# A nested seven-product scheme for one of the seven gate and up products, with the weights' scaling on VectorE

## The chip, the cores and the metric

The kernel runs on one core of one Trainium2 chip. The metric is the time of one execution on the device in microseconds (us). The kernel before has a median of 1574.11 us in three runs (1573.99 to 1574.41).

The engines are named as in the profile: PE is TensorE (matmuls; PEld its weight loads), DVE is VectorE, ACT is ScalarE, POOL is GpSimd, SP is SyncE, which issues the DMAs.

## The reference

For 2048 rows of 576 columns two branches are computed and mixed by a gate per row. A is attention with 32 heads of 18 columns in four chunks of 512 rows, with a memory carried from chunk to chunk; B is a feed-forward layer with a hidden width of 4608.

```python
def _B_ref(x, w_gate, w_up, w_down):
    return (_gelu(x @ w_gate) * (x @ w_up)) @ w_down

x = A_x
g = _sigmoid((x * gate_w).sum(-1, keepdims=True))
a = _A_ref(x, A_wq, A_wk, A_wv, A_wo, A_beta)
b = _B_ref(x, B_w_gate, B_w_up, B_w_down)
return g * a + (1 - g) * b
```

The change is in B's gate and up products, `x @ w_gate` and `x @ w_up`, and in what the two branches share.

## The kernel before

Every f32 operand is held as two 16-bit words, high and low, and a product is three matmuls (high by high, high by low, low by high) that add up in PSUM. ACT writes the high words (a copy to f16), POOL or DVE the low words (the value less its high word).

**Steps and blocks.** The hidden width is 36 tiles of 128, called f; the 2048 rows are four chunks of 512. A step `step(v)`, v = 0 to 71, does one f tile (f = v // 2) for one pair of chunks (p = v % 2): gate and up for two chunks. Four steps make a block (fb = v // 4, i4 = v % 4), with two f tiles. A step also holds a pair of attention heads (`scores`, `powers`, `pair_rows`, `turn_rows`, `values`) and a quarter of the down products of the block before (`chains`: `early` and `late`, six matmuls of 288 columns each into one bank, added to `acc` by DVE).

**Seven products.** The four products of a step (gate and up by two chunks), each over 512 inner columns, are formed with seven block products after Strassen's scheme (Winograd's form). Their weights are parts of `pairg`: A11, A22, S1, S2, S3, S4 and A12 by sums made on POOL (`sums_g`), from gate and up weights that were first scaled on POOL (`scale_g`, and `scale_d` for the down weights). The chunk side has its sums too (tile `xt`). Each product is six matmuls of 512 columns (`product`). The 64 columns beyond 512 are done by `rest` and `low_rests`. The S3 product starts each step in bank V (`first_product`), and DVE copies V out as g1 before the other products add to the bank.

**Order.** The instructions stand on each engine in the order in which the program issues them; each engine runs its own list in order and waits by semaphores. So the place of an instruction among the others of its engine is set by the place of its line in `step`. The helpers `weights_first`, `weights_high` (ACT), `weights_low` (POOL) and `weights_load` (SP) prepare the weights of the next tiles in fixed steps of a block: i4=1 and i4=3 have `sums_g`, i4=0 and 2 `scale_g`, i4=2 and 3 `scale_d`, `high_d`, `low_d`.

**Attention beside it.** `scores` puts four matmuls into PSUM; its pieces (`put`) let DVE add the mask, take the maximum and write the f32 probabilities' tile `pf`; `powers` is ACT's exp in place; `pair_rows` writes high and low words into the tile `ph`; `turn_rows` lets SP turn both by two DMA transposes into `pt`, which `values` multiplies. At a step's start, ACT runs the exps that the step before issued last.

**Other names.** `hh` are the high and low words of the hidden values (tiles of one pool for each parity of f), `gl` f32 hidden values in three homes, `raw` and `rawd` the f32 weights as loaded, `paird` the down weights' words, `acc` the f32 result, `ob` and `oh` the attention's result and its words (`result_high`, `result_low`), `squares` sums of squares that give the next weights' scales.

Of the kernel before, what the change touches and what calls it, by code (L numbers as in the profile page):

```python
# [18 lines left out]
P = 128  # L19
D = 576  # L20
F = 4608
H = 32
# [13 lines left out]
GB = 17  # L36
# [7 lines left out]
def kernel(ctx: ExitStack, tc: tile.TileContext, xs, wqk, wv, wo, wgu, wd, beta, out):  # L44
# [34 lines left out]

    def sum_squares(o, r):  # L80
        junk = wts.tile([P, KT * P], BF16, name="junk", tag="junk", bufs=1)
        dve.tensor_tensor_reduce(junk[:, : r.shape[1]], r, r, 1.0, 1e-30, OP.mult, OP.add, o)

    def act_square(o, r):
        junk = wts.tile([P, KT * P], BF16, name="junk", tag="junk", bufs=1)
        act.activation(junk[:, : r.shape[1]], r, AF.Square, accum_out=o)
# [208 lines left out]
    A11, A12, U4, A22, G4, S3, S1, UG, S2, S4 = 0, 2, 4, 5, 7, 8, 10, 12, 13, 15  # L295
    KW = KT * P

    def scale_g(f):
        if f >= NF:
            return  # L300
        for i in (1, 0):
            r = raw_g[f][:, i * KW : (i + 1) * KW]
            pool.tensor_scalar(r, r, scl[f // 2][0][:, 0:1], None, OP.mult)  # L303

    def parts_g(f, b):

        if f >= NF:
            return ()
        if b:
            return ((0, KW, S3), (KW, KW + 4 * P, S2))  # L310
        return ((KW, 2 * KW, A11), (2 * P, KW, A22))
# [6 lines left out]
    def sums_g(f):  # L318
# [6 lines left out]
        pool.tensor_tensor(g0, u0, g0, OP.subtract)  # L325
# [13 lines left out]

    def scale_d(f):  # L340
        r = raw_d[f]
        pool.tensor_scalar(r, r, scl[f // 2 + 1][0][:, 1:2], None, OP.mult)
# [44 lines left out]
    def form_sums(p, i, half, by=dve):  # L387
# [4 lines left out]
        if t is not None:  # L392
            hi, lo = (flat(t[:, 4 * k + j : 4 * k + j + 2]) for j in (0, 2))
        if half <= 0:
            by.tensor_tensor(r[o], r[a], r[b], OP.subtract)
        if half == 0 or half == 2:
            act.activation(hi, r[o], AF.Copy, scale=sc)
        if half == 1:
            dve.scalar_tensor_tensor(lo, r[o], sc, hi, OP.mult, OP.subtract)
# [19 lines left out]
    gh = cst.tile([P, 2, H], F32, name="gh")  # L419
# [14 lines left out]

    first, stay = ExitStack(), ctx.enter_context(ExitStack())
    with tc.tile_pool(name="prj", bufs=2, side="right", reuse_waits="tile") as pp:
        al = pp.tile([P, 4, 3], F32, name="al", bufs=1)
        nal = pp.tile([P, 4, 2], F32, name="nal", bufs=1)
        unq = pp.tile([P, 1], F32, name="unq", bufs=1)
# [4 lines left out]
        xt = [mp.tile([P, 12, L], F16, name="xt0", bufs=1)]  # L444
# [225 lines left out]
        with tc.manual_schedule(engines=ORDERED):  # L670
# [60 lines left out]
            for i in range(2):  # L731
                fold_squares(0, i)
# [68 lines left out]
            def beside_products(s, j):  # L801
# [4 lines left out]
                if s == 0:  # L806
                    if j == 0:
# [3 lines left out]
                        make_qk(3, pair_low)  # L811
                    if j == 1:
# [4 lines left out]
                        outscale(0, 2)  # L817
                        make_qk(4)
# [21 lines left out]
                if s == 2:  # L840
# [5 lines left out]
                    if j == 3:  # L846
                        load_sums(1)
                    if j == 8:
                        for f in range(3):
                            load_g(f)  # L850
                if s == 3:
# [3 lines left out]
                    if j == 1:  # L855
                        high_g(0, 1)
                        low_g(0, 1)
# [3 lines left out]
                    if j == 4:  # L861
                        load_g(3)
                    if j == 6:
# [8 lines left out]
                    if j == 8:  # L872
                        high_g(1, 1)
# [9 lines left out]
            for s in range(4):  # L883
# [26 lines left out]
                for j in range(9):  # L910
# [14 lines left out]
                    if s == 3 and j == 1:  # L925
# [3 lines left out]
                        xt.append(mp2.tile([P, 12, L], F16, name="xt1", bufs=1))  # L929
                        home.update(r=mp2)  # L930
                    beside_products(s, j)
# [25 lines left out]
    with tc.tile_pool(name="keep", bufs=2, side="right", reuse_waits="tile") as kp, ExitStack() as tail:  # L957
# [66 lines left out]
        def powers(a):  # L1024
# [5 lines left out]
            for qi in (3, 0, 2, 1):  # L1030
# [3 lines left out]
        def pair_rows(a, i):  # L1034

            p = prob[a]
            if i == 0:
                pairs16[a] = ap_.tile([P, 2, 10 * P], F16, name="ph", bufs=2)
# [3 lines left out]
            act.activation(h[:, 0, cols], p[:, cols], AF.Copy)  # L1042
            pool.tensor_tensor(h[:, 1, cols], p[:, cols], h[:, 0, cols], OP.subtract)  # L1043

        def turn_rows(a):
            prob.pop(a)
            t, h = turned_p[a], pairs16.pop(a)
            for i in range(2):
                sp.dma_start(t[:, 10 * i : 10 * i + 10], h[:, i], transpose=True)
# [34 lines left out]
        def result_high(gg):  # L1084
            ob = obs[gg]
            oh = ohs[gg] = ap_.tile([P, 2, 8, 4 * DH], F16, name="oh", bufs=1)
            act.activation(flat(oh[:, 0]), flat(ob), AF.Copy, scale=wsc[:, 3:4])

        def result_low(gg):
            hf, g = divmod(gg, H // 4)  # L1090
            ob, oh = obs.pop(gg), ohs.pop(gg)
            dve.scalar_tensor_tensor(flat(oh[:, 1]), flat(ob), wsc[:, 3:4], flat(oh[:, 0]), OP.mult, OP.subtract)
            d0 = g * 4 * DH
            for i in range(2):
                for a, b, c in ((d0, min(d0 + 4 * DH, 4 * P), i * 4 * P), (max(d0, 4 * P), d0 + 4 * DH, (4 + i) * P - i * 64)):
                    if a < b:
                        sp.dma_start(oas[hf][:, c + a : c + b].rearrange("(t p) c -> p t c", p=P),
                                     oh[:, i, :, a - d0 : b - d0])
# [19 lines left out]
        def chains(b, js):  # L1118
            for j in js:
                down(b, j // 2, j % 2)  # L1120
                if j % 8 == 7:
                    for ff in (2 * b, 2 * b + 1):
                        hp.pop((ff, j // 8))
                        if j == 31:
# [7 lines left out]
        def hidden_pair(f, c, t):  # L1132
            hh = hp[f, c] = (kp if f % 2 else mp2).tile([P, 2, L], F16, name=f"hh{f % 2}", bufs=6 - 2 * (f % 2))
# [40 lines left out]

# [22 lines left out]
        def act_squares(v):  # L1197

            fb, i4 = divmod(v, 4)
            todo = {0: ((fb + 1, 2 * fb, 2),),  # L1200
                    1: ((fb + 1, 2 * fb + 3, 0), (fb + 1, 2 * fb + 3, 1), (fb + 1, 2 * fb + 1, 2)),
                    2: ((fb + 2, 2 * fb + 4, 0), (fb + 2, 2 * fb + 4, 1))}
            todo = todo.get(i4, ()) if fb else ()
            if v == 4:
# [6 lines left out]
        def first_product(v):  # L1211
            f, p = divmod(v, 2)
            V = bank("V")
            product(V, f, S3, xt[p], 8, 10, True)
            g1 = gl_tile()
            dve.tensor_copy(g1, V)  # L1216
            return V, g1

# [14 lines left out]
        def step(v):  # L1233
# [12 lines left out]
            low = (k - 8) // 4 if k % 4 == 0 and 0 <= (k - 8) // 4 < H // 2 - 1 else None  # L1246
# [381 lines left out]
```

## Time and profile before

| | before |
|---|---|
| median of three runs | 1574.11 us |
| profiled execution, own time | 1574.38 us |
| its span in the trace | 1572.5 us |
| granted clock of PE | 1.00 |
| first step of block 0 | starts at 214.1 us |
| a block in the steady state | 73.15 us |
| its steps | 18.25 us each, the step i4=1 18.40 us |

The span is taken from the first to the last instruction in the trace, 1.9 us less than the execution's own time. A row of the timeline gives start, length, engine, line, operation, tiles and count; the length of a row with a count is from the first start to the last end, and matmuls overlap, so that PE's time is read from start to start. A row of a group gives the count, the busy time, the mean length of one in ns, and the idle time of the engine ahead of them with its releaser. The stretch shown in the prediction, from 750.87 us, is one steady step with i4=3; the steps ahead of it start at 714.22 (i4=1) and 732.62 (i4=2), the next one at 769.11 (i4=0).

### The profile page before, as it was taken

The page shows a single profiled execution, that of the slowest core. Times are in us where ns is not written, and L with a number is a line of the kernel's source. Part 1 is how long each engine was busy: PE and PEld are TensorE (multiplying, and loading weights), DVE is VectorE, ACT ScalarE, POOL GpSimd, SP SyncE. Part 2 cuts the span into 40 slices and gives each one's busy share as a digit, 9 for nine tenths or more (in the row PEclk, how much of TensorE's full clock was granted, in tenths as well). Part 3 has the DMA queues.
Part 4 walks back from the last instruction along what each step waited for, and adds up shares of the span by engine and source line. Part 5 has one row for each costly group of instructions (what it writes and reads, how often), then busy time and mean ns, then how long its engine had stood idle before and what let it go on. Part 6 is the DMA issues. An engine that isn't in the chain of part 4 may idle for free.

```text
span 1572.5 us, 32751 instructions
## 1 busy us (share of the span) xinstructions
PE 1562.6 (99%) x11914; PEld 929.0 (59%) x11914; DVE 1150.2 (73%) x3027; ACT 1172.7 (75%) x1983; POOL 1229.6 (78%) x1180
## 2 busy tenths in 40 slices
PE   9999999999999999999999999999999999999999
PEld 5665754555555555555555555555555555555577
DVE  6778974777777776767777777777777777776565
ACT  7566544988888888888888888888888888886421
POOL 4254765888888879898987888887879797788697
PEclk9999999999999999999999999999999999999999
DMA  6632432678788788978887888888797988884644
GB/s 228 215 123 101 149 120 72 111 129 128 134 135 136 127 151 125 139 127 138 129 131 129 139 133 137 133 134 152 131 136 129 144 129 136 129 127 91 135 108 136
DMA packets 472825, 209.88 MB, mean 133 GB/s; under 512 B 427688, under 2 KB 437416, under 8 KB 472152
## 3 DMA queue, kind: packets, MB, share of 16 engines
q1 hardware_dynamic: 472664, 207.80, 72.6%
q8 instruction: 93, 1.52, 0.4%
q14 instruction: 68, 0.56, 0.1%
HBM read 91.87 MB, written 27.26 MB: 76 GB/s over the span
## 4 chain that ended last, share of the span: by engine, by line
PE 95%; DVE 2%; ACT 1%; issue 1%; POOL 1%; DMA 0%; SPq 0%; ACTq 0%
PE dn L1108 27%; PE U L1148 18%; PE V L1148 12%; PE G L1148 12%; PE pv L1063 4%; PE dn L367 2%; PE U L1155 2%; PE st L360 2%; PE G L1160 1%; PE V L1160 1%; PE st L1016 1%; PE st L1468 1%; PE G L1155 1%; PE V L1155 1%; PE U L360 1%; PE dn L1016 1%
## 5 line engine op out<-in xcount | busy, mean ns | idle before, releaser
L1043 POOL TENSOR_TENSOR ph<-pf,ph 128x512 f16<-128x512 f32 (+1 forms) x256 | 353.6, 1402 | 173.2 <-ACT ph L1042 173.2
L1108 PE MATMUL dn<-paird,hh 128*128 128x288 f16 x3396 | 476.5, 286 | 0.0
L1148 PEld LDWEIGHTS <-pairg 128*128 128x128 f16 x3024 | 285.3, 98 | 305.1 <-issue 19.0
L1108 PEld LDWEIGHTS <-hh 128*128 128x128 f16 x3456 | 331.8, 98 | 153.7 <-issue 18.0
L1116 DVE SCALAR_TENSOR_TENSOR acc<-dn,ev,acc 128x288 f32<-128x288 f32 x534 | 274.4, 515 | 53.9 <-PE dn L1108 43.9
L1032 ACT ACTIVATE pf<-pf,mb,esc 128x512 f32<-128x512 f32 (+3 forms) x512 | 292.9, 642 | 7.0 <-POOL ph L1043 0.4
L1148 PE MATMUL U<-xt,pairg 128*128 128x512 f16 x864 | 210.0, 379 | 0.0
L1148 PE MATMUL G<-x,pairg 128*128 128x512 f16 x864 | 210.0, 379 | 0.0
L1135 POOL TENSOR_TENSOR hh<-gl,hh 128x512 f16<-128x512 f32 x144 | 164.3, 1160 | 19.1 <-ACT hh L1134 19.1
L338 POOL TENSOR_TENSOR pairg<-raw,pairg 128x640 f16<-128x640 f32 (+2 forms) x144 | 175.4, 1239 | 4.1 <-ACT pairg L334 4.1
L334 ACT ACTIVATE pairg<-raw 128x640 f16<-128x640 f32 (+2 forms) x144 | 90.0, 650 | 114.6 <-POOL raw L328 66.6
L1042 ACT ACTIVATE ph<-pf 128x512 f16<-128x512 f32 (+1 forms) x256 | 172.5, 721 | 0.0
L1293 DVE COPY gl<-U 128x512 f32<-128x512 f32 x72 | 49.8, 692 | 167.3 <-POOL hh L1135 150.8
L1019 DVE CUSTOM_DVE_ANT_0 pf<-st,mask 128x512 f32<-128x512 f32 (+1 forms) x256 | 157.2, 614 | 0.0
L303 POOL TENSOR_SCALAR raw<-raw,sc 128x640 f32<-128x640 f32 x72 | 135.7, 1896 | 0.0
L1019 DVE CUSTOM_DVE_ANT_0 pf<-dn,mask 128x256 f32<-128x256 f32 (+1 forms) x192 | 67.2, 375 | 81.7 <-PE dn L1016 81.7
L1138 ACT ACTIVATE gl<-gl,sc 128x512 f32<-128x512 f32 x144 | 96.6, 715 | 37.4 <-DVE gl L1319 19.3
L1148 PE MATMUL V<-xt,pairg 128*128 128x512 f16 x432 | 105.7, 381 | 0.0
L1148 PE MATMUL V<-x,pairg 128*128 128x512 f16 x432 | 104.8, 378 | 0.7 <-DVE gl L1216 0.7
L1148 PE MATMUL U<-x,pairg 128*128 128x512 f16 x432 | 105.0, 379 | 0.0
L1134 ACT ACTIVATE hh<-gl 128x512 f16<-128x512 f32 x144 | 82.6, 616 | 15.8 <-DVE gl L1130 15.7
L1063 PEld LDWEIGHTS <-pt 128*128 128x128 f16 x2560 | 83.4, 96 | 6.3
(316 smaller groups left out, 2642.6 us busy)
## 6 DMA issues: line engine op xcount, KB each, us to landing
raw<-in_wgu_dram SPq DMA_DIRECT2D x36, 640.0 KB
rawd<-in_wd_dram SPq DMA_DIRECT2D x36, 288.0 KB
qt<-qk SPq DMA_DIRECT2D x132, 72.0 KB
kt<-qk SPq DMA_DIRECT2D x132, 72.0 KB
qk<-stage SPq DMA_DIRECT2D x36, 256.0 KB
qt<-qk SPq DMA_DIRECT2D x132, 36.0 KB
kt<-qk SPq DMA_DIRECT2D x132, 36.0 KB
vp<-vstage SPq DMA_DIRECT2D x16, 296.0 KB
```

The lines of the kernel that those rows point to most:

```text
L303: pool.tensor_scalar(r, r, scl[f // 2][0][:, 0:1], None, OP.mult)
L338: pool.tensor_tensor(spot(f, *p, 1), raw_g[f][:, p[0] : p[1]], spot(f, *p, 0), OP.subtract)
L1019: dve.tensor_tensor_reduce(prob[a][:, COL[qi] : COL[qi + 1]], out[qi], mask[:, L - (qi + 1) * P :], 1.0, -3e38, OP.add, OP.max, mx[a][:, q ...
L1032: act.activation(r, r, AF.Exp, bias=b[:, qi : qi + 1], scale=esc[:, 0, c : c + 1])
L1042: act.activation(h[:, 0, cols], p[:, cols], AF.Copy)
L1043: pool.tensor_tensor(h[:, 1, cols], p[:, cols], h[:, 0, cols], OP.subtract)
L1063: pe.matmul(ov, pr[:, 10 * i + COL[qi] // P + kb], v[:, 4 * e + kb, c0 : c0 + VC], start=kb == 0 and i == 0, stop=kb == qi and i == 1)
L1108: pe.matmul(o[:, :NH], hh[:, a, q * P : (q + 1) * P], w[:, b, n * NH : (n + 1) * NH], start=i == 0, stop=i == 5)
L1116: dve.scalar_tensor_tensor(av, o[:, :NH], ev, av, OP.mult, OP.add)
L1135: pool.tensor_tensor(hh[:, 1], t, hh[:, 0], OP.subtract)
L1138: act.activation(t, o, AF.Gelu_apprx_tanh, scale=scl[f // 2][0][:, 2 + c : 3 + c])
L1148: pe.matmul(o, w[:, i, (a + k) * P : (a + k + 1) * P], x[:, b + k], start=start and k == 0 and i == 0 and b == h, stop=k == 1 and i == 1, ...
```

## The change

The S3 product of two f tiles of a block and one chunk pair is now done at once, as a 2 by 2 block product in its own right: seven products of 256 columns (three matmuls each) in place of two times six matmuls of 512 columns. Its weights (seven blocks: W00, W01, W11 and the sums WS1 to WS4, high and low words) lie in a new tile `nest`; the chunk side has seven blocks of 256 columns in `xt`. The pieces `nest(at, 0)` to `nest(at, 4)` stand in the steps i4=3 (for p = 0 of the next block) and i4=0 (for p = 1), the last one at the start of the following step. They gather their result in bank V for the even f and in an f32 tile `hold` for the odd f, whose g0 is then Y plus `hold`. Block 0 has no nest: its S3 product is 15 matmuls of 256 columns.

The parts that the prediction speaks of:

```diff
+    def nest_odd(b):
+        if b < NB:
+            nest_w[b] = nest_tile()
+            r = raw_g[2 * b + 1]
+            pool.tensor_tensor(nest_part(b)[1], r[:, KW : KW + 2 * P], r[:, : 2 * P], OP.subtract)
+
+    def nest_pairs(b, i, what):
+        if b >= NB:
+            return
+        a, r = nest_part(b)
+        src, o = ((a, W00), (r[:, P:], W11), (r, WS3), (a, WS2))[i]
+        n = src.shape[1]
+        hi, lo = (nest_w[b][:, (o + 7 * j) * P : (o + 7 * j) * P + n] for j in range(2))
+        if "h" in what:
+            act.activation(hi, src, AF.Copy)
+        if "l" in what:
+            pool.tensor_tensor(lo, src, hi, OP.subtract)
...
     def scale_d(f):
         r = raw_d[f]
-        pool.tensor_scalar(r, r, scl[f // 2 + 1][0][:, 1:2], None, OP.mult)
+        dve.tensor_scalar(r, r, scl[f // 2 + 1][0][:, 1:2], None, OP.mult)
...
             h = pairs16[a]
-            cols = (slice(6 * P, 10 * P), slice(0, 6 * P))[i]
-            act.activation(h[:, 0, cols], p[:, cols], AF.Copy)
-            pool.tensor_tensor(h[:, 1, cols], p[:, cols], h[:, 0, cols], OP.subtract)
+            cols = (slice(0, 6 * P), slice(6 * P, 10 * P))[i]
+            act.activation(h[:, cols], p[:, cols], AF.Copy)
+            pool.tensor_tensor(p.bitcast(F16)[:, cols], p[:, cols], h[:, cols], OP.subtract)
...
         def weights_first(fb, i4):
             n0 = 2 * fb
-            if i4 == 0 and fb:
-                scale_g(n0 + 1)
-            if i4 == 1 and fb:
+            if i4 == 0:
+                scale_g(n0 + 1, BACK)
+            if i4 == 1:
                 sums_g(n0 + 1)
-            if i4 == 2 and fb:
+            if i4 == 2:
                 scale_g(n0 + 2)
+                scale_g(n0 + 3, FRONT)
                 scale_d(n0)
-            if i4 == 3 and fb:
-                sums_g(n0 + 2)
+            if i4 == 3:
                 scale_d(n0 + 1)
+
+        def weights_nest(fb, i4, late):
+            if i4 == 2 and late:
+                sums_g(2 * fb + 2)
+                nest_odd(fb + 1)
+            if i4 == 3 and not late:
+                for i in range(2):
+                    nest_pairs(fb + 1, i, "hl")
+                nest_sums(fb + 1)
+            if i4 == 3 and late:
+                for i in (2, 3):
+                    nest_pairs(fb + 1, i, "hl")
...
+            if n == 0:
+                nest_product(b, A, WS3, XT3, p, True)
+                dve.tensor_copy(h1, A)
+                nest_product(b, B, W00, X00, p)
+            if n == 1:
+                nest_product(b, A, W11, XT4, p)
+                dve.tensor_copy(h0, A)
+                dve.tensor_copy(A, B)
+            if n == 2:
+                nest_product(b, B, W01, X10, p)
+                nest_product(b, A, WS2, XT2, p)
+                dve.tensor_tensor(h0, A, h0, OP.add)
+            if n == 3:
+                nest_product(b, A, WS1, XT1, p)
+                dve.tensor_tensor(h1, A, h1, OP.add)
+            if n == 4:
+                nest_product(b, A, WS4, X11, p)
...
             if fb:
                 weights_high(fb, i4)
                 weights_low(fb, i4)
+                weights_nest(fb, i4, True)
...
             product(Y, f, S4, x2_, 2, 6)
             rest(Y, f, UG, x2_, (0,) if fb else (0, 1))
+            nest(at, 0)
             some(fb - 1, late[:1])
...
-            some(fb - 1, late[1:])
+            some(fb - 1, late[1:2])
+            nest(at, 1)
+            some(fb - 1, late[2:])
             if low is not None:
                 result_low(low)
             if on(k - 1):
                 values(2 * k - 2)
+            nest(at, 2)
...
             if on(k):
                 puts[2 * k + 1] = scores(2 * k + 1)
+            nest(at, 3)
```

Beside these: `pairg` has 15 parts instead of 17; the result's low words lie in `ob`, and `result_low` moves from i4=0 to i4=3; `hh` tiles come from one list of eight homes; `powers` and `pair_rows` take their parts in another order; the squares of a block's first `rawd` move from i4=0 to i4=1; `fold_squares(0, ...)` stands later in the prologue; the output stage holds fewer tiles ahead.

On POOL, step i4=3 of a steady block, from the sums or the nest's words to the last words of the step. Before (`raw` are weights' sums, `ph` probabilities' words):

```order
L324 TENSOR_TENSOR raw<-raw 128x256
L325 TENSOR_TENSOR raw<-raw 128x256
L326 TENSOR_TENSOR raw<-raw 128x256
L327 TENSOR_TENSOR raw<-raw 128x256
L328 TENSOR_TENSOR raw<-raw 128x128
L342 TENSOR_SCALAR rawd<-rawd,sc 128x576
L1043 TENSOR_TENSOR ph<-pf,ph 128x512
L1043 TENSOR_TENSOR ph<-pf,ph 128x768
L338 TENSOR_TENSOR pairg<-raw,pairg 128x640
L338 TENSOR_TENSOR pairg<-raw,pairg 128x512
L350 TENSOR_TENSOR paird<-rawd,paird 128x576
```

And of the changed kernel, the same step (L377 are the nest's low words, L384 to L387 its sums, L1141 the probabilities' low words):

```order
L377 TENSOR_TENSOR nest<-raw,nest 128x256
L377 TENSOR_TENSOR nest<-nest 128x128
L384 TENSOR_TENSOR nest<-nest 128x128
L385 TENSOR_TENSOR nest<-raw,nest 128x128
L386 TENSOR_TENSOR raw<-nest,raw 128x128
L387 TENSOR_TENSOR raw<-raw 128x128
L1141 TENSOR_TENSOR pf<-pf,ph 128x768
L1141 TENSOR_TENSOR pf<-pf,ph 128x512
L342 TENSOR_TENSOR pairg<-raw,pairg 128x384
L342 TENSOR_TENSOR pairg<-raw,pairg 128x512
L399 TENSOR_TENSOR paird<-rawd,paird 128x576
L377 TENSOR_TENSOR nest<-nest 128x256
```

The scaling has left the list and the weights' sums have moved to the step ahead; four of the nest's sums and two of its low words stand at the place of the sums, and the low words of WS3, the last row, behind all other words of the step.

On DVE, step i4=2 of a steady block, from the copy of X to Y to what follows the last piece of a `put`. Before:

```order
L1257 COPY U<-G 128x512
L1116 SCALAR_TENSOR_TENSOR acc<-dn,ev,acc 128x288
L1019 ISA pf,mx<-st,mask 128x384
L1019 ISA mx 128x1
L1293 COPY gl<-U 128x512
```

And of the changed kernel:

```order
L1426 COPY U<-G 128x512
L1215 SCALAR_TENSOR_TENSOR acc<-dn,ev,acc 128x288
L1117 ISA pf,mx<-st,mask 128x384
L1117 ISA mx 128x1
L304 TENSOR_SCALAR raw<-raw,sc 128x1280
L304 TENSOR_SCALAR raw<-raw,sc 128x2x256
L391 TENSOR_SCALAR rawd<-rawd,sc 128x576
L1475 TENSOR_TENSOR gl<-U,hold_11823 128x512
```

Three scalings stand between the last piece and g0, and g0 is a sum with `hold` instead of a copy.

More of the change, by code (lines that the diff above doesn't have):

```diff
@@ L35 @@
 VC = 2 * DH + 1
-GB = 17
+GB = 15
 MC = DH + 1
@@ L1217, in first_product, with nest_product, nest @@
             return V, g1
+        nested, holds = {}, {}
+        def nest_product(b, o, i, j, p, start=False):
+            w, x = nest_w[b], x_block(p, j)
+            for n, (c, d) in enumerate(((0, 0), (0, 1), (1, 0))):
+                pe.matmul(o, w[:, (7 * c + i) * P : (7 * c + i + 1) * P], x[d], start=start and n == 0, stop=n == 2,
+                          skip_group_check=True)
+        def nest(at, n):
+            if at is None:
+                return
+            b, p = at
+            if n == 0:
+                nested[at] = bank("V")
+                holds[p] = kp.tile([P, L], F32, name=f"hold{p}", bufs=1)
+            B, A = (nested[at][:, i * HX : (i + 1) * HX] for i in range(2))
+            h0, h1 = (holds[p][:, i * HX : (i + 1) * HX] for i in range(2))
+            if n == 0:
+                nest_product(b, A, WS3, XT3, p, True)
[14 more added lines that the diff above has]
+                nest_product(b, A, WS4, X11, p)
         ends, puts = [], {}
@@ L1252, in step @@
             act_squares(v)
-            V, g1 = ahead.pop(v) if v in ahead else first_product(v)
+            at = (fb + 1, 0) if i4 == 3 and fb + 1 < NB else (fb, 1) if i4 == 0 and fb else None
+            if not fb:
+                V, g1 = ahead.pop(v) if v in ahead else first_product(v)
+            elif i4 < 2:
+                if on(k - 2):
+                    values(2 * k - 3)
+                nest((fb, p), 4)
+                V, g1 = nested.pop((fb, p)), gl_tile()
+                dve.tensor_copy(g1, V)
+            else:
+                V, g1 = bank("V"), holds[p]
+                product(V, f, A22, x2_, 0, 4, True)
             X, Y = bank("G"), bank("U")
@@ L1259, in step @@
                 last_sum(1, 1)
+                for i in range(2):
+                    nest_pairs_x(1, i)
             if v == 1:
@@ L1540 @@
             NT = 8
-            for t in range(turned_n, 11):
+            for t in range(turned_n, 9):
                 turned(t)
```

202 lines of the change are left out of this document (144 added, 58 removed).

## The prediction

> **What bounds the kernel now.** I read the shares of the page first, then the chain that ended last, then TensorE's waits.
>
> ```profile
> PE 1562.6 (99%) x11914; PEld 929.0 (59%) x11914; DVE 1150.2 (73%) x3027; ACT 1172.7 (75%) x1983; POOL 1229.6 (78%) x1180
> PE 95%; DVE 2%; ACT 1%; issue 1%; POOL 1%; DMA 0%; SPq 0%; ACTq 0%
> ```
>
> TensorE is busy 99% of the span and carries 95% of the chain. Its waits by releaser add up to a few microseconds, each of them met once; the only one in the feed-forward loop is
>
> ```profile
> PE V L1148 <- DVE gl L1216: 0.7, 1, 0.7
> ```
>
> So before the change a matmul removed is time removed. But the other engines are at 73 to 78%, and POOL's work comes in bursts, so the steady state has to be read step by step. One block of two f tiles is four steps (i4 = 0 to 3). I use the block around 751 us; its step i4=3 runs from 750.87 to 769.11. The window view of that step (span, then busy time and instructions of PE, PEld, DVE, ACT, POOL, then clock) says:
>
> ```profile
> 750.87:769.11 18.24, 18.24 (x149) 10.60 (x147) 13.06 (x37) 14.44 (x24) 16.37 (x16) 1.00 0.71 118
> ```
>
> PE never stops, POOL is busy 16.37 of 18.24 us, and the clock is full. PE's timeline of the step:
>
> ```profile
> 750.87 1.47 PE L1148 MATMUL V<-xt,pairg 128*128 128x512 f16 x6
> 752.17 1.46 PE L1148 MATMUL G<-x,pairg 128*128 128x512 f16 x6
> 757.51 0.90 PE L1108 MATMUL dn<-paird,hh 128*128 128x288 f16 x6
> 758.25 1.46 PE L1148 MATMUL G<-x,pairg 128*128 128x512 f16 x6
> 762.32 0.38 PE L1016 MATMUL st<-kt,qt 54*128 54x512 f16 x2
> 762.69 1.65 PE L1108 MATMUL dn<-paird,hh 128*128 128x288 f16 x12
> 765.47 0.38 PE L1155 MATMUL U<-x,pairg 128*128 128x512 f16 x1
> 765.68 2.40 PE L1108 MATMUL dn<-paird,hh 128*128 128x288 f16 x18
> ```
>
> From start to start, six 512-column matmuls take 1.30 us (216 ns each) and six of 288 columns 0.74 us (123 ns).
>
> **Term 1, matmuls.** For blocks 1 to 17 the S3 product, the first row above, leaves all four steps: 24 x 216 ns = 5.2 us a block. The nested product puts 2 x 21 matmuls of 256 columns there. No row has that width. By columns from 512 it is 108 ns, from 288 it is 109; the ceiling is the 123 ns of 288 columns. I take 109: 4.6 us. Saved: 0.6 us a block (0.0 at the ceiling), 17 x 0.6 = 10 us. Block 0 goes from 6 x 216 to 15 x 109 ns in four steps, +0.34 us each, +1.4 us. Net about -9 us if nothing waits. It also shifts PE within the block: i4=1 and 2 lose 1.30 us each (about 17 us long), while i4=3 and 0 keep their length, the nest's pieces standing late in i4=3.
>
> **Term 2, POOL in step i4=3.** The new weights of the nested product (sums and seven pairs of high and low words) are made in i4=2 and 3, just ahead of their use. POOL executes in order. The third matmul of nest piece 0 needs the low words of WS3, and in the changed order these stand behind POOL's whole list of step i4=3. When is that list done? It starts where it starts today, with the probabilities' low words after ScalarE's exps and high words:
>
> ```profile
> 751.01 2.29 ACT L1032 ACTIVATE pf<-pf,mb,esc 128x512 f32<-128x512 f32 x4
> 753.21 1.35 ACT L1042 ACTIVATE ph<-pf 128x512 f16<-128x512 f32 x2
> 753.90 2.77 POOL L1043 TENSOR_TENSOR ph<-pf,ph 128x512 f16<-128x512 f32 x2 [1.64 <-ACT ph L1042]
> 758.85 0.73 POOL L324 TENSOR_TENSOR raw<-raw 128x256 f32<-128x256 f32 x1
> 759.66 0.72 POOL L325 TENSOR_TENSOR raw<-raw 128x256 f32<-128x256 f32 x1
> 769.27 1.28 POOL L350 TENSOR_TENSOR paird<-rawd,paird 128x576 f16<-128x576 f32 x1
> ```
>
> POOL starts 3.0 us into the step; with the 768 columns first, 3.2. I keep this start: ScalarE's own list for the shorter i4=2 fills it, so exps do not come earlier. The durations, by form:
>
> ```profile
> L1043 POOL TENSOR_TENSOR ph<-pf,ph 128x768 f16<-128x768 f32 x128 | 210.5, 1644 | 0.0
> L1135 POOL TENSOR_TENSOR hh<-gl,hh 128x512 f16<-128x512 f32 x144 | 164.3, 1160 | 19.1 <-ACT hh L1134 19.1
> L338 POOL TENSOR_TENSOR pairg<-raw,pairg 128x512 f16<-128x512 f32 x36 | 41.8, 1160 | 0.0
> L338 POOL TENSOR_TENSOR pairg<-raw,pairg 128x384 f16<-128x384 f32 x36 | 33.4, 928 | 0.0
> L350 POOL TENSOR_TENSOR paird<-rawd,paird 128x576 f16<-128x576 f32 x36 | 46.1, 1281 | 6.3 <-ACT paird L346 6.3
> L324 POOL TENSOR_TENSOR raw<-raw 128x256 f32<-128x256 f32 x36 | 26.2, 727 | 0.2
> L328 POOL TENSOR_TENSOR raw<-raw 128x128 f32<-128x128 f32 x36 | 16.3, 454 | 0.0
> ```
>
> In the order of the new list: probabilities 1.64 + 1.16; hidden low words 2 x 1.16; nest low words of 256 and 128 columns 0.73 + 0.45; nest sums 4 x 0.45, with four gaps of 0.08 (758.85 to 759.66 for 0.73); probabilities 2.80; pairg 0.93 + 1.16; paird 1.28; at last the WS3 low words 0.73. That is 15.3 us, less some 0.2 for neighbours that overlap in the timeline: done about **18.3 us** into the step.
>
> PE wants them early. Today the U product closes at 765.68, 14.8 us into the step; without the S3 product that is 13.5, and the third nest matmul stands 0.2 behind it: **13.7 us**. The difference, **4.6 us**, is a wait in every block, with late chains, values, scores and the block's end queued behind it on PE. Today POOL ends its list as late (769.27 + 1.28, 19.7 us after the step's start) and nobody notices, since those words serve the next block. The time is a constant one, not made good by the step's end: the next exps hang on the gelu of this step, and that on PE. Scaling by VectorE does take 1.7 us out of this list, and the sum has it out. Bounds of this term: 4.0 (ScalarE half a microsecond early) to 6.5 (ScalarE late by a microsecond, and the locks below). Sixteen steps have it (blocks 1 to 16 make the nest of the next): 16 x 4.6 = 74 us.
>
> **Term 3, block 0 to 1.** Step v=3 has no late chains between the nest's pieces; copies and adds of 256 columns, each half of a 512-column VectorE copy, lie bare between matmuls, and WS3 comes late there too.
>
> ```profile
> L1257 DVE COPY U<-G 128x512 f32<-128x512 f32 x72 | 50.0, 695 | 2.6 <-PE G L1148 2.6
> ```
>
> Five of 0.35 to 0.7 us, and 1.5 for the weights: 3 to 5 us, bounds 0 and 8. I take 4.
>
> **Term 4, VectorE's new scales.** No f32 tensor_scalar from SBUF to SBUF of this size is in the trace. By the copy's 695 ns per 512 columns, the 2368 columns of i4=2 are 3.2 us; at half of that, 1.6. They stand ahead of g0's add, which S1 on PE needs, where VectorE is idle today:
>
> ```profile
> 757.81 0.69 DVE L1293 COPY gl<-U 128x512 f32<-128x512 f32 x1 [2.38 <-POOL hh L1135]
> ```
>
> So 1.6 are hidden, 3.2 stick out by 0.8, and PE would wait for some of it. There is a second price, a lock between VectorE and POOL. Beside VectorE's tensor_scalar at 177.96, two POOL rows (640 and 384 columns) that take 1.43 and 0.93 alone took 3.48:
>
> ```profile
> L338 POOL TENSOR_TENSOR pairg<-raw,pairg 128x640 f16<-128x640 f32 x72 | 103.3, 1434 | 4.1 <-ACT pairg L334 4.1
> 177.96 1.41 DVE L228 TENSOR_SCALAR x<-x,xr 128x4608 f16<-128x4608 f16 x1
> 178.02 3.48 POOL L338 TENSOR_TENSOR pairg<-raw,pairg 128x640 f16<-128x640 f32 x2 [2.41 <-ACT pairg L334]
> ```
>
> That is 1.1 us more than alone, while VectorE's instruction ran on for 1.3. In i4=2 a scale may have to let a POOL row of up to 1.64 us go first. Range 0 to 1.4 us a block; I take 0.2, since most of it lies in the idle 2.38 us.
>
> **Term 5, low words in place.** The probabilities' low words now lie in pf itself, so VectorE's next mask-and-max into that buffer waits for the DMA transposes out of it. Their issue in i4=0:
>
> ```profile
> 774.05 5.92 SPq L1049 DMA_TRANSPOSE pt<-ph  x2
> ```
>
> It ends 10.9 us into that step; the scores (762.32, 11.4 us into their step) come 0.8 to 1.3 us earlier than now, and one chain later PE wants the bank that VectorE is to empty. Nothing if they land at once, 1.1 us if they need the 1.4 us more that I allow; 0.2 a block.
>
> The rest costs nothing: squares and exps only change places on ScalarE, which is not waited for; the tail's smaller buffers lie beside PE work; the later folds may give 0.7 us in the prologue.
>
> **The sum**, against the profiled execution's 1574.4 (span 1572.5; the median 1574.1 is 0.3 below): 1574.4 - 9 + 74 + 4 + 17 x 0.4 = **1650 us**.
>
> [...]
>
> **The rivals.**
> - POOL is in time (faster). If POOL's list began 4.6 us earlier, or WS3's place in it were no matter, only the matmuls would count: 1574.4 - 9 = **1565**. For it: POOL loses all its scaling:
>
> ```profile
> L303 POOL TENSOR_SCALAR raw<-raw,sc 128x640 f32<-128x640 f32 x72 | 135.7, 1896 | 0.0
> L342 POOL TENSOR_SCALAR rawd<-rawd,sc 128x576 f32<-128x576 f32 x36 | 62.0, 1722 | 0.0
> ```
>
> These are 198 us, and it gains some 58: 17 nests of 4 x 0.73 + 5 x 0.45 us, less 36 x 0.5 by narrower low words and 17 x 0.73 by a sum left out. The point that decides is 13.7 us into i4=3. Against it: the start of the list is set by exps, not by POOL's load, and fifteen microseconds stand ahead of WS3. Chance 0.15.
> - The wait is there but 1 to 2.5 us, by ScalarE running ahead in i4=2: 1574.4 - 9 + 4 + 16 x 1.75 = **1597**. Chance 0.15.
> - Locks and the transposes bite fully: +0.6 in i4=3, 1.2 more in i4=2 and 0.9 more in i4=0, 16 x 2.7 over the sum, **1693**. For it: the rows at 178 us. Against it: VectorE's idle time. Chance 0.10.
> - The change doesn't do what it says: a 256-column matmul costs 123 ns. Then term 1 is +1 instead of -9: 1660 with the waits, 1575 without them. Chance of the latter 0.03.
>
> **The numbers.** The forecast, waits of 4 to 6 us in i4=3, has 0.57. Its own range is 1635 to 1675. The range that should hold the time 8 times in 10 takes in the partial wait and the locks: 1585 to 1695. A measurement of this kernel can tell about 0.2% from no change. Faster by more 0.15, within 0.03, slower by more 0.82.
>
> **What would show it.** TensorE's waits should have a row for nest behind POOL's low words (L377) of about 4.6 us x 16, and POOL's timeline should have its last-but-one nest row ending 18 us after i4=3's start; steps i4=1 and 2 should be near 17 us. Term 1 is read from the starts of the nest's rows (109 ns). If that wait is under 1 us, term 2 is wrong, and POOL's start or ScalarE's place is where to look. If waits stand behind the scales (L304, L391) or behind transposes, terms 4 or 5 were too small.

## The result and the profile after

| | before | after |
|---|---|---|
| median | 1574.26 us (four runs, 1573.99 to 1574.54) | 1745.96 us (four runs, 1744.47 to 1746.91) |
| span of the profiled execution | 1572.5 us | 1745.2 us |
| granted clock of PE, mean | 1.00 | 0.976 |

The changed kernel is slower: the ratio of the times is 1.109, with a 95% interval of 1.1076 to 1.1104. That is 172 us, where 76 were forecast, and outside the range.

The shares of the engines, on the page of the changed kernel:

```profile
PE 1613.6 (92%) x12256; PEld 977.2 (56%) x12256; DVE 1292.8 (74%) x3256; ACT 1183.1 (68%) x2057; POOL 1120.5 (64%) x1218
```

PE went from 99% to 92%, so it now waits; yet its busy time grew by 51 us with less work to do, which no count of matmuls explains. POOL is less busy than before. The waits of PE, by releaser (total, times, longest):

```profile
PE V L1346 <- POOL nest L377: 68.4, 16, 4.8
PE V L1346 <- DVE hold L1361: 19.9, 34, 0.8
PE U L1249 <- DVE gl L1475: 5.9, 16, 0.4
PE G L1249 <- DVE gl L1230: 5.6, 33, 0.2
PE dn L1207 <- DVE mx L1117: 4.0, 5, 1.1
PE dn L1207 <- DVE acc L1215: 3.0, 15, 0.2
```

The first row is term 2 of the prediction, sixteen times. The second was in no term: the copy of A out of the bank, twice a block. (The profile counts 0.58 us of idleness for each; from start to start it costs 0.75 us.)

Measured from the end of one step's scores to the next, the steady steps last, by their means, 18.24 us (i4=1, before 18.40), 17.74 (i4=2, 18.25), 25.74 (i4=3, 18.24) and 20.70 (i4=0, 18.26): a block went from 73.15 to 82.42 us. By stretches, the way up to the end of the first step with attention grew by 16.0 us (the prologue ahead of the first block product by 7.8 of them), the 63 steps behind it by 148.7, and the way from there to PE's last matmul by 7.7.

One long wait on PE's timeline, and POOL's at the same place:

```profile
1249.73 0.38 PE L1256 MATMUL U<-x,pairg 128*128 128x512 f16 x1
1249.95 0.38 PE L1346 MATMUL V<-xt,nest 128*128 128x256 f16 x2
1254.83 0.28 PE L1346 MATMUL V<-xt,nest 128*128 128x256 f16 x1 [4.50 <-POOL nest L377]
1255.70 0.80 PE L1346 MATMUL V<-xt,nest 128*128 128x256 f16 x3 [0.58 <-DVE hold L1361]
1256.29 0.92 PE L1207 MATMUL dn<-paird,hhd 128*128 128x288 f16 x3
1257.01 0.92 PE L1207 MATMUL dn<-paird,hhr 128*128 128x288 f16 x3
...
1258.82 0.49 PE L1346 MATMUL V<-xt,nest 128*128 128x256 f16 x3
1259.15 0.53 PE L1207 MATMUL dn<-paird,hhd 128*128 128x288 f16 x3
1259.52 0.53 PE L1207 MATMUL dn<-paird,hhr 128*128 128x288 f16 x3
```

```profile
1239.72 2.98 POOL L1141 TENSOR_TENSOR pf<-pf,ph 128x768 f16<-128x768 f32 x2 [0.79 <-ACT ph L1140]
...
1247.64 0.46 POOL L387 TENSOR_TENSOR raw<-raw 128x128 f32<-128x128 f32 x1
1248.06 2.88 POOL L1141 TENSOR_TENSOR pf<-pf,ph 128x768 f16<-128x768 f32 x2
1250.90 2.02 POOL L342 TENSOR_TENSOR pairg<-raw,pairg 128x384 f16<-128x384 f32 x2
1252.88 1.27 POOL L399 TENSOR_TENSOR paird<-rawd,paird 128x576 f16<-128x576 f32 x1
1254.11 0.67 POOL L377 TENSOR_TENSOR nest<-nest 128x256 f16<-128x256 f32 x1
```

The step begins at about 1236.5. POOL's list starts 3.2 us later and its WS3 words are done at 1254.78, 18.3 us later; PE's third nest matmul, due at 1250.17, starts at 1254.83. Both ends are the forecast's, 18.3 and 13.7. What was not forecast follows in the same rows: the fourth matmul stops again, for VectorE's copy, and the down products behind it go from start to start in 0.72 us by threes (240 ns each), before they return to 0.37 (122 ns). In the window view of PE (the window and its length, PE's busy time and matmuls, the granted clock, the share of the DMA engines and GB/s):

```profile
1252.00:1254.00 2.00, 0.00 (x0) 1.00 0.73 164
1254.00:1256.00 2.00, 0.58 (x3) 0.76 0.37 82
1256.00:1258.00 2.00, 2.00 (x11) 0.50 0.77 214
1258.00:1260.00 2.00, 2.00 (x20) 0.89 0.46 179
1260.00:1262.00 2.00, 1.94 (x35) 1.00 0.00 0
```

After 4.5 us without a matmul PE runs on at half its clock for 3.4 us (what the three windows with 0.76, 0.50 and 0.89 lack of the full clock, taken twice). This is one part of how its busy time grew; the experiment that fills the wait, below, puts it at about half of the 51 us.

### The profile page after: what moved, and what is told of

Its sections match the earlier page's. It is cut to its first block, busy times and chain, and to the rows that moved or that the text cites. A ratio compares the mean times of both kernels' runs of the same rounds, so it can differ in the third digit from the quotient of the medians.

```text
span 1745.2 us, 34088 instructions
## 1 busy us (share of the span) xinstructions
PE 1613.6 (92%) x12256; PEld 977.2 (56%) x12256; DVE 1292.8 (74%) x3256; ACT 1183.1 (68%) x2057; POOL 1120.5 (64%) x1218
## 5 line engine op out<-in xcount | busy, mean ns | idle before, releaser
L1141 POOL TENSOR_TENSOR pf<-pf,ph 128x768 f16<-128x768 f32 (+1 forms) x256 | 368.2, 1438 | 418.9 <-ACT ph L1140 408.9
L1207 PE MATMUL dn<-paird,hhr 128*128 128x288 f16 x2124 | 341.8, 295 | 3.8 <-DVE acc L1215 2.0
L1130 ACT ACTIVATE pf<-pf,mb,esc 128x256 f32<-128x256 f32 (+3 forms) x512 | 292.9, 642 | 5.5 <-issue 0.4
L1207 PEld LDWEIGHTS <-hhr 128*128 128x128 f16 x2160 | 214.6, 101 | 103.8 <-issue 13.3
L1207 PE MATMUL dn<-paird,hhd 128*128 128x288 f16 x1272 | 213.1, 294 | 3.4 <-DVE mx L1117 2.4
L1346 PE MATMUL V<-xt,nest 128*128 128x256 f16 x714 | 121.6, 285 | 92.6 <-POOL nest L377 68.4
L1140 ACT ACTIVATE ph<-pf 128x768 f16<-128x768 f32 (+1 forms) x256 | 172.4, 720 | 0.0
L342 POOL TENSOR_TENSOR pairg<-raw,pairg 128x384 f16<-128x384 f32 (+2 forms) x144 | 156.4, 1108 | 12.9 <-ACT pairg L338 12.9
L1207 PEld LDWEIGHTS <-hhd 128*128 128x128 f16 x1296 | 128.6, 100 | 58.3 <-issue 8.3
L1236 POOL TENSOR_TENSOR hhr<-gl,hhr 128x512 f16<-128x512 f32 x67 | 79.9, 1203 | 23.4 <-ACT hhr L1235 23.4
```

What stands on the lines that cost most here:

```text
L342: pool.tensor_tensor(spot(f, *p, 1), raw_g[f][:, p[0] : p[1]], spot(f, *p, 0), OP.subtract)
L1130: act.activation(r, r, AF.Exp, bias=b[:, qi : qi + 1], scale=esc[:, 0, c : c + 1])
L1140: act.activation(h[:, cols], p[:, cols], AF.Copy)
L1141: pool.tensor_tensor(p.bitcast(F16)[:, cols], p[:, cols], h[:, cols], OP.subtract)
L1207: pe.matmul(o[:, :NH], hh[:, a, q * P : (q + 1) * P], w[:, b, n * NH : (n + 1) * NH], start=i == 0, stop=i == 5)
L1236: pool.tensor_tensor(hh[:, 1], t, hh[:, 0], OP.subtract)
```

## The experiments

Each time below is that of a single run. The kernel before, run beside each, took 1573.99 to 1574.93 us; the four runs of the changed kernel differ by up to 2.4 us, so a difference of that size between two of these times shows nothing by itself.

### The place of the WS3 words in POOL's list

First, the nest's last words ahead of the weights' low words:

```diff
                 turn_rows(2 * k - 1)
+            if fb and i4 == 3:
+                weights_nest(fb, i4, True)
...
                 weights_low(fb, i4)
-                weights_nest(fb, i4, True)
+                if i4 != 3:
+                    weights_nest(fb, i4, True)
```

Second, also ahead of the odd head's probabilities, directly behind the nest's sums (ScalarE's high words move to the same places; the last hunk is as above, and a step without an odd head has the words too):

```diff
                 powers(2 * k - 1)
+                if fb and i4 == 3:
+                    weights_nest(fb, i4, True)
                 pair_rows(2 * k - 1, 0)
```

> The low words of WS3 stand behind the probabilities' low words but ahead of the three last weights' rows (0.93 + 1.16 + 1.28 us). If their place in POOL's list makes PE wait, TensorE's wait behind the nest's low words falls from 4.65 to about 1.3 us a block, 16 x 3.4 = 54 us. If TensorE's clock falls to a half because it had been idle over 4 us, that goes too, 1.4 us a block, 22 us more: about 1670. Without a share of the clock 1692. If POOL as a whole is late, the wait only moves: about 1745.

> The low words of WS3 and WS2 stand directly behind the nest's sums, ahead of the odd head's probabilities. By the place in POOL's list the wait behind the nest is gone (16 x 4.65 = 74 us, and 22 of the clock): about 1650. If the odd head's low words, now 2.5 us later in that step, reach their DMA transposes too late, VectorE waits for these at the next step's start and gives back 1 to 2 us a block: 1666 to 1680.

Measured: 1682.99 us and 1657.46 us. The row of waits behind the nest in the first:

```profile
PE V L1346 <- POOL nest L377: 16.4, 14, 1.3
```

The single wait fell by just the three rows of POOL that were passed, to at most 1.3 us; in the second the row is gone, and with it 88 us. The wait on POOL is thus a matter of place, as argued. In the first the time lies between the two figures for the clock: its mean clock is 0.99, not 1.00. In four blocks this wait (1.45 us from start to start) and the copy's 0.75 directly behind it were still followed by the half clock, in most not. In the second, a part came back as a wait of the nest's piece 3 for VectorE's sums:

```profile
PE V L1346 <- DVE hold L1370: 6.2, 12, 0.8
```

### The copy between A and B

```diff
                 nest_product(b, A, WS3, XT3, p, True)
-                dve.tensor_copy(h1, A)
                 nest_product(b, B, W00, X00, p)
+                dve.tensor_copy(h1, A)
```

> Only the order in the nest's first piece is changed: the copy of A out of bank V stands behind B's three matmuls instead of ahead of them. If B's first matmul waits for that copy because both lie in one bank, 34 waits of 0.75 us go: about 1746 - 25 = 1721. If the matmuls are slow there for another reason (VectorE's turn, clock), nothing changes: 1745.

Measured: 1730.05 us; of the 34 waits for the copy one of 0.5 us is left. So B's first matmul waited, by the program's semaphores, for a copy of the other half of its bank; whether the chip itself would need that wait is not shown. The step i4=0 gained 0.79 us, the step i4=3 only 0.17, and 9 us of the forecast are missing: there the half clock lasted longer instead. The trace's record of the clock has it for 6.8 us in 14 of the 16 blocks here, in the changed kernel for 6.8 us in 7 and for 3.4 us in 9 (mean clock 0.969 against 0.976). The two orders together, the second kernel above with this edit:

> The early WS3 words and the copy behind B together. If the two costs are apart from each other (the wait on POOL with its half clock, and the wait on VectorE's copy), they add up: 1657.5 - 33 x 0.75 = 1633. If the copy's place only matters beside the long wait, it stays near 1657.

Measured: 1633.29 us. Once the long wait is gone, the copy's whole price shows: 24.2 us below the second kernel of the first experiment.

### Filling the wait

```diff
+                if b > 1 and p == 0:
+                    for _ in range(40):
+                        pe.matmul(A, nest_w[b][:, WS3 * P : (WS3 + 1) * P], x_block(p, XT3)[0], start=True, stop=False,
+                                  skip_group_check=True)
                 nest_product(b, A, WS3, XT3, p, True)
```

> In the sixteen steps with the long wait TensorE repeats the nest's first matmul 40 times (40 x 0.109 = 4.4 us) while POOL works; each repeat starts the sum anew. If the half clock after the wait comes from TensorE's idleness, it stays at 1.00 and the kernel gets faster by about 16 x 1.4 = 22 us, to about 1724, although it does more. If it is not the idleness, the time stays at 1745 or grows.

Measured: 1728.64 us, 17 us less than the changed kernel with 640 matmuls more. PE's timeline and the clock behind the same place:

```profile
1241.08 4.53 PE L1362 MATMUL V<-xt,nest 128*128 128x256 f16 x40
1245.44 0.81 PE L1346 MATMUL V<-xt,nest 128*128 128x256 f16 x3
1246.84 0.49 PE L1346 MATMUL V<-xt,nest 128*128 128x256 f16 x3 [0.58 <-DVE hold L1365]
1247.16 0.53 PE L1207 MATMUL dn<-paird,hhd 128*128 128x288 f16 x3
```

```profile
1246.00:1248.00 2.00, 1.42 (x11) 1.00 0.71 173
1248.00:1250.00 2.00, 2.00 (x29) 1.00 0.81 236
```

The forty matmuls take 4.36 us from start to start (109 ns each, the value taken in term 1), POOL's words come as late as ever, and the chains behind run at full clock. PE's busy time is 1658.3 us, which less 640 matmuls of 109 ns is 25 us below that of the changed kernel. So the half clock was the price of PE's idleness, and a wait of this length costs more than itself. Its price is 1.5 us a block, 24 us in all, more than the 17 us won: the steady step i4=3 lasts 24.22 us (25.74 without the filling), but for one of 29.43 us, in which PE waits 3.75 us for VectorE's masks. In the sixteen waits of the changed kernel, after 3.3 to 4.8 us of idleness, the slow matmuls (240 ns for 288 columns) begin 1.0 to 1.9 us after PE resumed and end 3.2 to 6.5 us after it. But shorter idleness was enough at times, as the four blocks above show (1.45 and 0.75 us from start to start).

### Parts of the change alone, in the kernel before

The weights' scaling on VectorE (two words changed, `pool` to `dve`, in `scale_g` and `scale_d`); the output stage's sums written over their own inputs; the probabilities' low words in place (with the changed order of the parts); and the first with the third.

```diff
-            pool.tensor_tensor(s1, a21, a22, OP.add)
-            pool.tensor_tensor(s2, s1, a11, OP.subtract)
-            pool.tensor_tensor(s3, a11, a21, OP.subtract)
-            pool.tensor_tensor(s4, a12, s2, OP.subtract)
+            pool.tensor_tensor(a22, a21, a22, OP.add)
+            pool.tensor_tensor(a21, a11, a21, OP.subtract)
+            pool.tensor_tensor(a11, a22, a11, OP.subtract)
+            pool.tensor_tensor(a12, a12, a11, OP.subtract)
...
-            pool.tensor_tensor(h[:, 1, cols], p[:, cols], h[:, 0, cols], OP.subtract)
+            pool.tensor_tensor(p.bitcast(F16)[:, cols], p[:, cols], h[:, cols], OP.subtract)
```

> The kernel before, with only the weights' scaling moved from POOL to VectorE (at the same places, 2 x 640 and 576 columns). If the scales delay g0's copy and the sums behind it, PE waits 0.5 to 0.9 us in i4=2 as in the changed kernel: 1574 + 17 x 0.5 to 0.9 = 1583 to 1589. If VectorE's idle 2.4 us and POOL's shorter list cover them, 1574.

> The kernel before, with only the output stage's sums written over their own inputs (as many tiles ahead as before). If POOL's longer turn by pair (the gaps between dependent sums and the wait for ScalarE, 8.3 instead of 7.3 us in the traces) is what the tail lost, about +5 to +8 us: 1580. If it was the smaller number of tiles ahead, 1574.

> The kernel before, with only the probabilities' low words written over the probabilities, and the parts in the changed order. If VectorE's next mask-and-max waits for the DMA transposes and PE for it, 0.2 to 1 us a block or more: 1578 to 1592. If the transposes land in time, 1574.

> The kernel before with low words in place (1617.4 alone) and scales on VectorE (1579.7 alone) together. If in-place low words cost so much there because POOL's scales hold the odd head's low words back until the transposes land too late, the scales on VectorE take most of that away: 1580 to 1595. If the two costs are independent, they add up: 1574 + 43 + 5.5 = 1623.

Measured: 1579.69, 1581.19, 1617.39 and 1605.99 us.

- Scales: half of the 5.5 us lies ahead of the first step with attention, where PE waits 1.5 us for VectorE's `vstage`; the steady step i4=2 grew by just 0.13 us. There VectorE's idle time nearly covers it.
- Sums in place: the tail grew by 6.2 us, of the 7.7 in the changed kernel. POOL's timeline of one pair in this kernel:

```profile
1547.41 0.73 POOL L1444 TENSOR_TENSOR pairg<-pairg 128x256 f32<-128x256 f32 x1
...
1549.83 0.73 POOL L1447 TENSOR_TENSOR pairg<-pairg 128x256 f32<-128x256 f32 x1
1551.30 2.26 POOL L1459 TENSOR_TENSOR x<-pairg,x 128x512 f16<-128x512 f32 x2 [0.74 <-ACT x L1458]
...
1555.74 0.72 POOL L1444 TENSOR_TENSOR pairg<-pairg 128x256 f32<-128x256 f32 x1
```

  From pair to pair it takes 8.33 us. Before, the sum rows stand at 1542.57 and 1549.88 (7.3 us), and POOL passes from the last sum to the low words without a wait. The smaller number of tiles ahead is not needed to explain the tail.
- Low words in place: the largest surprise, 43 us. VectorE's waits for it:

```profile
DVE pf L1019 <- DMA pt<-pf: 95.2, 48, 5.2
```

  VectorE stands for the transposes 48 times, up to 5.2 us, and PE behind VectorE 25 times, 27.1 us in all; behind the three longest of these waits of PE (3.2 to 3.4 us) the clock fell to half. With the scales on VectorE the same row falls to 31.6 us in 15 waits, and the time to 1605.99, 17 us below the plain sum of both. So POOL's shorter list does bring the low words earlier (a step's last ones end on average 3.3 us earlier in i4=0 and 4.1 in i4=2), and in the kernel before the two parts are not independent. In the changed kernel PE's whole wait of this kind is 4.0 us.

### The rest of the prologue, the tail and i4=2

On the kernel with both orders (1633.29 us): `nest_pairs_x(0, 1)` and `nest_sums_x(1)` moved to the end of the last projection's products; then, added to it, the tail's first two sums in columns of their own and, in i4=2, the weights' sums on POOL, the nest's first difference and VectorE's scaling of 2 x 256 columns behind g0; and last, the same without that move in i4=2.

```diff
-                scale_g(n0 + 3, FRONT)
...
             if i4 == 2 and late:
+                scale_g(2 * fb + 3, FRONT)
                 sums_g(2 * fb + 2)
...
                 dve.tensor_tensor(g0, Y, g1, OP.add)
+                if i4 == 2:
+                    weights_nest(fb, i4, True)
```

> As both orders together, and two pieces of the chunk side of the nest (VectorE's low words of 1024 columns, POOL's four sums of 256 columns) stand at the end of the projection's products instead of ahead of the words that TensorE waits for there. If these two made the prologue 8 us longer (two waits and a stretch at half clock at 210 us), 1633 - 5 to 8 = 1625 to 1628. If the longer prologue has other causes, 1633.

> As the one with the prologue moved; the output stage's first two sums go to columns of their own again, so that fewer of them hang on one another and ScalarE starts earlier (up to -7), and in i4=2 VectorE scales the 2 x 256 columns behind g0's sum instead of ahead of it (16 waits of 0.5 us, -6 to -8). Together 1626 - 8 to - 15: 1611 to 1618. If VectorE's scales are not what g0 waits for, only the tail's part: 1619.

> As the one with the tail's sums in columns of their own, but with VectorE's 2 x 256 columns scaled ahead of g0's sum again and POOL's sums back at their place in i4=2. If the irregular long waits behind the transposes in the run before came from that later place in POOL's list, they go, and the tail's gain stays: 1630.9 - 5.5 = 1625. If they come from the tail's or the prologue's edits, 1634 or so.

Measured: 1630.92, 1635.60 and 1626.56 us.

- Prologue: of the two waits (2.0 us behind `x`, 2.2 behind `phi`) 0.5 us are left, but a new one took their place at the first step,

```profile
PE G L1247 <- DVE stage L614: 3.1, 1, 3.1
```

  and only 2.4 us were won, no more than single runs differ by; in the trace the way up to the end of the first step with attention is 1.7 us shorter. What stood there must be done somewhere before the first product.
- In i4=2 with the scaling moved, the undisturbed steps lasted 17.15 instead of 17.74 us, so VectorE's scale cost PE 0.6 us there. But some steps of that kind took up to 23.1 us, and PE's wait behind the masks grew from 5.3 to

```profile
PE dn L1205 <- DVE mx L1115: 16.1, 16, 3.4
```

  VectorE's waits on the transposes came back (31.2 us in 19 waits, against 8.3 in 4). The move causes them, as without it they are gone again (PE's wait behind the masks is 4.2 us); by what path is not shown, as the low words themselves end no later in the step (11.85 us after its start, 11.84 without the move). The tail's gain stays: the last kernel is the fastest with the nest, 3.3% above the kernel before. No version tried beats the kernel before.

## Why the prediction was wrong

The sign and the main mechanism were right; the size was not, because waits of PE that the prediction costed at nothing, or nearly so, made up more than half of the loss.

- **Term 1** (matmuls, -9 us): right. The nest's matmuls take 109 ns from start to start. But the shift between the steps was read wrongly: -1.30 us in i4=1 and 2 and nothing in i4=3 and 0 makes -2.6 us a block, not -0.6. Six of a block's 42 nest matmuls stand at the start of i4=1, 21 in i4=0 and 15 in i4=3, so that i4=1 loses only 0.65 us and i4=0 grows by 1.0. So one of the signs to look for failed: i4=1 was to be near 17 us and lasts 18.24 (0.5 us of it are short waits, named below).
- **Term 2** (WS3, 4.6 us a block, 74 us): right. Sixteen waits, 4.5 us by the profile in the block shown, 68.4 us in all; its start, its end and its position on PE came out to a tenth of a microsecond. Moving the words up the list removed just what was passed.
- **The failing step** is the sum: it took term 2's wait at its own length, added 0.4 us a block for terms 4 and 5, and held that nothing else in the steady block would make PE wait. The block grew by 9.3 us, and term 2's wait is 4.3 of them. The two largest costs that it left at nothing are the half clock behind the wait, 1.5 us a block (shown by filling the wait), and the copy out of the bank, 1.5 us a block (shown by changing the order). The half clock could not be read in the profile before, where the granted clock is 1.00 and no steady wait existed; the prediction could have asked what idleness does to the clock.
- **Term 3** (copies): it counted VectorE's 256-column copies as bare only in step v=3, "no late chains between the nest's pieces". The copy stands not between the pieces but within the first one, between the third and the fourth matmul, and waits for the bank and not for the columns. Twice a block, 24 us in all once the long wait is gone. The way from block 0's start to the first step with attention grew by 8.2 us, where terms 1 and 3 had 5.4.
- **Term 4** (0.2 us a block): too small. It shows on VectorE's timeline of an i4=2 step (its first row is two instructions, 1280 and 512 columns), with POOL's rows beside it:

```profile
1305.17 2.43 DVE L304 TENSOR_SCALAR raw<-raw,sc 128x1280 f32<-128x1280 f32 x2
1307.52 1.41 DVE L391 TENSOR_SCALAR rawd<-rawd,sc 128x576 f32<-128x576 f32 x1
1308.86 0.68 DVE L1475 TENSOR_TENSOR gl<-U,hold 128x512 f32<-128x512 f32 x1
1303.97 3.35 POOL L1141 TENSOR_TENSOR pf<-pf,ph 128x768 f16<-128x768 f32 x2 [4.58 <-ACT ph L1140]
1307.28 1.33 POOL L1236 TENSOR_TENSOR hhr<-gl,hhr 128x512 f16<-128x512 f32 x1
```

  The three scalings take 3.7 us from the first's start to that of `gl`; g0 ends at 1309.5 and PE's S1 starts with it, 0.52 us late, and 0.27 us more than before go behind the next scores: 0.8 us a block, within the bounds of 0 to 1.4, but not at the end that was taken. Undoing a part of it gave 0.6 back. By these rows what was mis-sized is not the work but how long VectorE and POOL hold each other up: at 238 us, with POOL idle, the scaling of 576 columns took 0.51 us, here 1.41, and it ends 0.32 us behind POOL's row (1308.61). POOL's two rows before it take 3.35 us, where the prediction's rows sum to 2.80. The kernel before shows it on VectorE too: L268, 2 columns wide, took 0.70 us at 357.62, ending 0.03 us behind the POOL row beside it (L325, done at 358.29), and 0.16 at its shortest. By the shortest rows of the run (0.89 us for 1280 columns, 0.51 for 576) the three would take some 1.9 us, an estimate, and fit into VectorE's idle 2.38 us. In i4=3 POOL was held up little: its first two rows there, in the stretch shown above, took 2.98 us for 2.80, and its list ended when forecast; no run shows the 0.6 us that the rival with locks has there.
- **Term 5** (0.2 us a block): about right for the changed kernel (4.0 us of PE's waits), for a reason that the prediction had not, and so by luck: with the scales on VectorE the low words are ready earlier (shown in the kernel before). In the kernel before the same edit costs 43 us.
- **Left out altogether:** A11's product, which now comes so soon behind a step's scores that its bank is still being read (33 times 0.33 us from start to start); some four short waits a block, of 0.1 to 0.2 us, for VectorE's sums in the nest; the prologue (7.8 us; the prediction had 0 to -0.7); and the tail, costed at nothing because it lay "beside PE work", where the sums' chain made POOL the slower of the two (6.2 us, shown).

The waits of a block so add up: 4.3 for WS3, 1.5 of clock, 1.5 of copies, 0.8 behind the scales, 0.65 for A11, and by difference some 1.1 of small ones, against 0.6 saved: 9.3 us, the growth measured.

What stays open: how much of the remaining 52 us of the best version could go. By its trace 16 us lie ahead of the end of the first step with attention, 36 in the 63 steps behind it (the steps i4=0 last 20.4 us and i4=3 19.0 on average, the other two no longer than before) and none in the tail. Low words in a tile of their own were not tried.

## What to carry to other kernels

When a matrix engine that never waited is made to wait, price the wait with what follows it: here 4.5 us of idleness cost about 1.5 us more at half clock, and 40 useless matmuls in each of the sixteen gaps made the kernel 17 us faster. Here a product split into pieces that share one bank waited 0.75 us, twice a block, for a copy out of that bank, though other columns were copied; issue the other half's matmuls first. Words that are needed first belong first in the list of the in-order engine that makes them, and a buffer that is reused in place inherits the wait of its last reader, a DMA included (VectorE stood up to 5.2 us for the transposes here): count it from the landing.

## What the runs showed of the hardware that was not expected

- In the changed kernel the half clock came with each of the sixteen waits of PE of 3.3 to 4.8 us, behind one of 2.2 us (at 210.24) and behind one of the three of 1.4 us in the tail (at 1725.81); behind those of 1.83 and 1.97 us (at 46.10 and 160.03) it did not, nor behind one of 2.22 us in the run with the tail's sums in columns of their own and i4=2's scaling moved (at 1084.36; six matmuls of 288 columns behind it take 0.73 us from start to start). The changed kernel's record of the clock has it in stretches of 3.4 or 6.8 us, and a wait's length does not tell which: two waits of 4.50 us, at 759.96 and at 923.98 us, were followed by one of 3.4 and one of 6.8. In the second, a row 5.1 us after PE resumed is still slow (three matmuls in 0.72 us from start to start):

```profile
923.98 0.39 PE L1346 MATMUL V<-xt,nest 128*128 128x256 f16 x1 [4.50 <-POOL nest L377]
929.07 0.92 PE L1207 MATMUL dn<-paird,hhd 128*128 128x288 f16 x3
929.79 0.92 PE L1207 MATMUL dn<-paird,hhr 128*128 128x288 f16 x3
```

- The scaling on VectorE took longer beside POOL's rows, and the trace has this as busy time, not as a wait: one of 576 columns took 0.51 us with POOL idle and 1.41 beside POOL's rows (at 1307.52), and one of 1280 columns, an f32 tensor_scalar from SBUF to SBUF, 0.89 us at its shortest, a rate about twice that of VectorE's copies out of PSUM (0.69 us for 512). Over the whole run their means are 1.07 and 1.13 us:

```profile
L391 DVE TENSOR_SCALAR rawd<-rawd,sc 128x576 f32<-128x576 f32 x36 | 38.3, 1068 | 0.0
L304 DVE TENSOR_SCALAR raw<-raw,sc 128x1280 f32<-128x1280 f32 x19 | 21.3, 1126 | 0.2 <-POOL sc L278 0.2
```

  Half the columns take nearly the same time; 34 of the 36 rows of 576 columns and all 19 of 1280 lie beside POOL's for at least half their length. No run took POOL away to measure this by itself.
